# Attention maxima of a head: rounded and split on GpSimd, turned later, copied by ScalarE

## The chip, the cores and the metric

The kernel runs on one core of a Trainium2 chip. Its time is that of one execution on the device, in microseconds (us); lower is better. The engines are called as the profile calls them: PE (TensorE; PEld is its loading of weights), DVE (VectorE), ACT (ScalarE), POOL (GpSimd) and SP (SyncE, which here only issues transfers).

## The reference

A block of a transformer on one sequence of 2048 tokens with 448 features: a layer norm modulated by a condition, attention with 16 heads of 28 features, and behind it a gated MLP with a mixing of the tokens. Only the attention is touched.

```
q, k, v = heads of h @ wqkv                 # 16 heads, 2048 x 28 each
scores  = (q @ k^T) * 28 ** -0.5            # 2048 x 2048 for each head
p       = exp(scores - max) / sum           # softmax over the keys
o       = p @ v
x       = x + ga * (o @ wo)
```

## The kernel before

The attention goes head by head, and within a head over 16 key tiles of 128 keys, two at a time (a *pair*, function `pair`). The scores are made with the keys on the partitions and 512 queries on the columns (`s_mm`, tile `st_ps`), ACT turns them into `P` by an exponential, and PE multiplies `P` with `V` (`pv_mm`, tile `o_ps`) one pair later. What has to be known before a head's scores are taken is the greatest score of each query, since the exponential works on score minus maximum.

These maxima are made about 20 key tiles ahead (`LEAD`). For each block of 128 queries, `m_mm` makes the product with 512 keys (tile `mt`) and DVE reduces it to one column of `pm` (L754). In heads 1 to 13 (`RAW`) the first 512 queries go another way: their scores are made with the keys on the partitions (`r_mm`, tile `rt`), ACT copies them to SBUF as raw tiles (`rawA`, `rawB`, `rawC`), DVE folds them into a running maximum `rmax` (L801), and `r_turn` turns that by PE and reduces it into the first four columns of `mxv` (L809). Once the maxima are known, `r_neg` (L813, L817) spreads them over the partitions as `rneg`, POOL adds it to the raw tiles (`r_sub`, L820), and ACT takes the exponential from there.

`m_max` finishes a head: one reduction of `pm` gives the negated maxima `mxv` (128 x 16), and three more write their rounded part and the remainder (`mxp`, both in a type with fewer bits for PE). `m_fin` turns `mxp` by PE (L775, tile `mtp`), DVE copies the 32 x 128 result to `nt` (L778), and SP sends it into rows 84 and 85 of `qst`, the query operand of the scores, so that the product with the keys comes out with the maximum already subtracted. POOL has work beside this: sums of blocks of the mixing weights (`ws_op`, L957 and L952), whose loads and stores go through SP.

Each engine works in the order in which the program writes its instructions. That order is written out by hand: `ORDERS` has one letter for each step of a pair (r raw score, p products with V, s score, m maximum product, | the events of the second key tile), and tables `events` and `late` hold what is run at a key tile: `events` of the first tile at the pair's start, `late` of it right behind the products with V. A planner (`Clock`) with estimates of how long a bank of PSUM is held chooses the bank of each product.

`m_max` and `m_fin` of head h stand at key tile 16h - 4 of the whole row of tiles, that is, two pairs ahead of the head's own first tile. In a head after 13, `m_fin` stood one tile later in `events`.

Of the kernel before, what the change touches and what calls it, by code (L numbers as in the profile page):

```python
# [8 lines left out]
F32 = mybir.dt.float32  # L9
F32R = mybir.dt.float32r  # L10
AF = mybir.ActivationFunctionType
ALU = mybir.AluOpType
AX = mybir.AxisListType
# [6 lines left out]
NT = S // 128  # L20
# [67 lines left out]
def tile_adaln_mha_gmlp(ctx, tc, x, wqkv, wo, w_in, w_spT, b_sp, w_out, cT, w_mod, out):  # L88
    nc = tc.nc
    ctx.enter_context(tc.manual_schedule())  # L90
    pe, dve, act, pool, sp = nc.tensor, nc.vector, nc.scalar, nc.gpsimd, nc.sync
# [48 lines left out]
    def sub(eng, dst, a, hi):  # L140
        eng.tensor_tensor(out=dst, in0=a, in1=hi.bitcast(F32), op=ALU.subtract)  # L141
# [101 lines left out]
    def bank(name):  # L243
        k = mode[0](name) if mode[0] else banks[0]
        banks.remove(k)
        banks.append(k)
        return ring.tile([128, 512], F32, name=name, tag=f"b{k}")
# [6 lines left out]
    def load_mod(pair, eng):  # L254
        for k in range(4):
            n = 2 * D if k < 3 else 512
            wms[pair, k] = wm = e1.tile([128, 2 * D], F32, name="wm", tag=("wm", "wm", "raw")[pair], bufs=4)[:, :n]
            eng.dma_start(wm, w_mod[:, pair, 2 * D * k : 2 * D * k + n])
            if k < 3:
                wms[pair, k] = wm.rearrange("p (a b) -> p a b", b=D)  # L260
# [43 lines left out]
    for r0, r1, a, o in ((0, 128, 0, 3), (0, 64, 3, 1), (64, 128, 3, 1)):  # L304
        b = a + r0 // 64
# [239 lines left out]
    order = [(0, 0), (0, 3), (2, 2), (2, 5), (1, 1), (3, 0), (1, 4), (5, 2), (4, 1), (6, 6), (6, 7)]  # L545
# [103 lines left out]
    for g in range(1, NG):  # L649
        if g == 3:  # L650
# [4 lines left out]
            npool = att.enter_context(tc.tile_pool(name="npool", bufs=2))  # L655
# [73 lines left out]
    RAW = range(1, 14)  # L729
# [13 lines left out]
    pms = {}  # L743

    def m_mm(j, kb):
        h, t = divmod(j, NT)
        mt = bank("mt")
        pe.matmul(  # L748
            mt, qst[h % 3][:, t * 128 : (t + 1) * 128], kst[h % 3][:, kb * 512 : (kb + 1) * 512], start=True, stop=True
        )  # L750
        if h not in pms:
            pms[h] = npool.tile([128, NT, 4], F32, name="pm")
        clock.read("dve", 0.598)
        dve.tensor_reduce(out=pms[h][:, t, kb : kb + 1], in_=mt, axis=AX.X, op=ALU.max)  # L754

    mxs = {}

    def m_max(h):

        r = 4 if h in RAW else 0  # L760
        if h not in mxv:
            mxv[h] = npool.tile([128, NT, 2], F32, name="mxv")
        mx = mxv.pop(h)
        clock.spend("dve", 0.5)
        dve.tensor_reduce(out=mx[:, r:, 0], in_=pms.pop(h)[:, r:, :], axis=AX.X, op=ALU.max, negate=True)
        mxs[h] = npool.tile([128, 2, NT], F32R, name="mxp")
        dve.tensor_reduce(out=mx[:, :, 1].bitcast(F32R), in_=mx[:, :, 0:1], axis=AX.X, op=ALU.max, negate=True)
        dve.tensor_reduce(out=mxs[h][:, 0, :], in_=mx[:, :, 0:1], axis=AX.X, op=ALU.max)
        with nc.allow_low_precision(reason="the low part of a split, as the other splits write it"):
            dve.tensor_reduce(out=mxs[h][:, 1, :], in_=mx, axis=AX.X, op=ALU.add)  # L770

    def m_fin(h):
        mx = mxs.pop(h)
        tp = bank("mtp")
        pe.transpose(tp[0 : 2 * NT, 0:128], mx.bitcast(F32).rearrange("p a b -> p (a b)"), ident)  # L775
        nt = npool.tile([2 * NT, 128], F32, name="nt", bufs=1)
        clock.read("dve", 0.3)
        dve.tensor_copy(nt, tp[0 : 2 * NT, 0:128])  # L778
        sp.dma_start(qst[h % 3][84:86, :].bitcast(F32), nt[:, :])

    mxv, seen, rmax, rneg = {}, [], [], []
# [6 lines left out]
    def r_mm(u):  # L788
        st = score("rt", *divmod(u, NT), 0)
        b = clock.read("act", 0.477, hold=u % NT > 0)  # L790
        act.activation(raw_tile(u), st, AF.Copy)  # L791
        if u % NT:
            seen.append((u, st, b))

    def r_max():
        while seen:
            u, st, b = seen.pop(0)
            if not rmax:
                rmax.append(stage2.tile([128, 512], F32, name="rmax", tag="ql"))
            clock.read("dve", 0.6, *b)  # L800
            dve.tensor_tensor(out=rmax[0], in0=st, in1=raw_tile(u - 1) if u % NT == 1 else rmax[0], op=ALU.max)  # L801

    def r_turn(h):
        tp = bank("rtp")
        for t in range(4):
            pe.transpose(tp[:, t * 128 : (t + 1) * 128], rmax[0][:, t * 128 : (t + 1) * 128], ident)  # L806
        mxv[h] = npool.tile([128, NT, 2], F32, name="mxv")
        clock.read("dve", 0.62)
        dve.tensor_reduce(out=mxv[h][:, 0:4, 0], in_=tp.rearrange("p (a b) -> p a b", b=128), axis=AX.X, op=ALU.max, negate=True)  # L809

    def r_neg(h):
        st = bank("st_ps")
# [19 lines left out]
    def s_mm(u, qb):  # L832
        st = score("st_ps", *divmod(u, NT), qb)
        clock.ready[u] = clock.read("act", 0.477)[1]
        s_exp(u, qb, st)

    def x_exp(u):
        clock.ready[u] = clock.spend("act", 0.477)
        s_exp(u, 0, raw_tile(u))
# [4 lines left out]
    def pv_mm(u):  # L844
        h, kt = divmod(u, NT)
        if kt == 0:
            otile[h] = ps_o.tile([128, 512], F32, name="o_ps", tag="o")
        for qb in range(4):
            pe.matmul(  # L849
                otile[h][32 * qb : 32 * qb + 32, :], V[:, kt, h, :], ptiles.pop((u, qb)), start=kt == 0, stop=kt == NT - 1  # L850
            )
# [120 lines left out]

    LEAD = 20
    NU = H * NT
    events, late = {}, {}

    def at(slot, fn, *a, when=events):
        when.setdefault(slot, []).append((fn, a))

    for h in range(H):  # L980
        if h >= 2:
            at(h * NT - LEAD - 10, load_head, h)
        e0 = (h + 1) * NT
        at(e0 + 1, n_copy, h)
        at(e0 + 2, n_sum, h)
        at(e0 + 4, n_recip, h)
        at(e0 + 6, n_bcast, h)
        at(e0 + 8, n_mul, h)
        at(e0 + 9, n_scatter, h)
        at(h * NT + NT - LEAD, m_max, h)  # L990
        at(max(h * NT + NT - LEAD, -2) + (h > RAW[-1]), m_fin, h, when=events if h > RAW[-1] else late)
    for h in RAW:
        at(h * NT - 6, r_turn, h, when=late)
        at(h * NT - 1, r_neg, h)
# [74 lines left out]
    def m_first():  # L1069
        j, kb = first[done[0]]  # L1070
        m_mm(j, kb)
        done[0] += 1
        if done[0] >= 4 * NT and kb == 3:
            for when in (events, late):
                for e in [e for e in sorted(when) if e <= j - 3 - LEAD]:
                    for fn, a in when.pop(e):
                        fn(*a)
# [33 lines left out]
    def run(when, u):  # L1111
        for fn, a in when.pop(u, []):
            fn(*a)

    ORDERS = {6: "rrpm|smsmssmsmsm", 8: "rrpm|smmsmmsmsmsm"}

    def pair(u):
        ss = [[(v, qb) for qb in range(1 if v // NT in RAW else 0, 4)] if v < NU else [] for v in (u, u + 1)]
        S_, M_, R_ = ss[0] + ss[1], m_work[u] + m_work[u + 1], r_work[u] + r_work[u + 1]
        X_ = [v for v in (u, u + 1) if v < NU and v // NT in RAW]  # L1120
        xat = [len(R_)] * 2
        if X_:
            order = ORDERS[8 if len(M_) > 6 else 6]
        else:
            lead = 1 if M_ else 4
            order = "r" * len(R_) + "s" * lead + "p" + "ms" * (4 - lead) + "|" + "ms" * 4 + "m" * len(M_)
        n_o = 0

        def exps():
            while X_ and n_o >= xat[-len(X_)]:  # L1130
                x_exp(X_.pop(0))

        run(events, u)
        exps()
        for c in order + "s" * len(S_) + "r" * len(R_) + "m" * len(M_):
            if c == "p":
                if u > 0:
                    pv_mm(u - 2)
                    pv_mm(u - 1)
                    clock.pause((u - 2, u - 1))  # L1140
                run(late, u)
            elif c == "|":
                run(events, u + 1)
            elif c == "s" and S_:
                s_mm(*S_.pop(0))
                n_o += 1
                exps()
            elif c == "r" and R_:
                r_mm(R_.pop(0))
                n_o += 1  # L1150
                exps()
                if not R_:
                    r_max()
            elif c == "m" and M_:
                m_mm(*M_.pop(0))
        assert not X_ and not seen
        run(late, u + 1)
# [102 lines left out]
    h = H - 1  # L1260
# [310 lines left out]
    for s in range(2):  # L1571
        for six in (False, True):
            prev = None
            for n in [n for n in range(s, NP, 2) if PRODUCTS[n][1] or not six]:
                c, _, new, _ = PRODUCTS[n]
# [184 lines left out]
    order = free[0:3] + [free[6]] + free[3:6]  # L1760
# [68 lines left out]
```

## Time and profile before

| | us |
|---|---|
| median of 3 runs | 1352.79 |
| lowest, highest | 1352.58, 1353.44 |
| the profiled execution | 1353.0 |
| its span, first to last instruction | 1351.2 |

| engine | busy us in the span | share |
|---|---|---|
| PE | 1344.5 | 100% |
| DVE | 1082.2 | 80% |
| ACT | 908.5 | 67% |
| POOL | 604.2 | 45% |

The attention's pairs run from about 151 us to 837 us of the span. A matmul's end is modelled in these records, so that PE counts as busy even in short waits; where it waits is seen from the starts of its instructions and from the idle time of the weight loads. Figures in brackets at a row's end are idle time of that engine just before, and what ended it.

### The profile page before, as it was taken

How to read it: one execution, taken by the hardware profiler on the slowest of the kernel's cores; microseconds unless marked ns; L12 is line 12 of the kernel's file. 1: busy time of each engine (PE TensorE's matmuls, PEld its weight loads, DVE VectorE, ACT ScalarE, POOL GpSimd, SP SyncE). 2: the span in 40 equal slices, each digit the busy share in tenths (PEclk: the TensorE clock that was granted, in tenths of full speed). 3: DMA queues.
4: the chain of work that ended last, by engine and by line, in shares of the span. 5: the costliest groups of instructions: out<-in, count | busy, mean ns of one | idle time of the engine just before them, and what ended most of it. 6: DMA issues, size and time to landing. Idle time of an engine off the chain costs nothing.

```text
span 1351.2 us, 20695 instructions
## 1 busy us (share of the span) xinstructions
PE 1344.5 (100%) x6945; PEld 939.2 (70%) x6945; DVE 1082.2 (80%) x1777; ACT 908.5 (67%) x1687; POOL 604.2 (45%) x521
## 2 busy tenths in 40 slices
PE   9999999999999999999999999999999999999998
PEld 8888655555555555555555555988998888888898
DVE  7798889999999999999999960851379798889582
ACT  6623789999999999999997779363234653444221
POOL 2134428987888779788787761100141000000000
PEclk9999999999999999999999999999999999999999
DMA  8465614455345525553434222533102443435842
GB/s 296 135 175 181 211 57 127 135 150 150 112 121 151 144 86 136 146 155 109 113 80 119 83 80 66 189 119 136 63 9 89 125 114 102 118 103 178 269 157 82
DMA packets 92870, 174.68 MB, mean 129 GB/s; under 512 B 16536, under 2 KB 31770, under 8 KB 90218
## 3 DMA queue, kind: packets, MB, share of 16 engines
q1 hardware_dynamic: 90046, 169.06, 41.7%
q10 hardware_dynamic: 2718, 4.30, 0.9%
q8 instruction: 55, 0.90, 0.3%
q14 instruction: 51, 0.42, 0.1%
HBM read 111.71 MB, written 56.82 MB: 125 GB/s over the span
## 4 chain that ended last, share of the span: by engine, by line
PE 97%; DVE 2%; ACT 0%; issue 0%; POOL 0%; DVEq 0%; ACTq 0%
PE acc L1605 19%; PE o_ps L849 17%; PE mt L748 15%; PE st_ps L785 14%; PE z_ps L1497 5%; PE z_ps L1329 5%; PE pq L413 4%; PE rt L785 4%; PE wo_ps L1194 3%; PE y_ps L1685 2%; PE y_ps L1683 2%; PE pv L395 2%; PE y_ps L1684 2%; DVE pm L754 1%; PE rtp L806 1%; PE tp L191 1%
## 5 line engine op out<-in xcount | busy, mean ns | idle before, releaser
L754 DVE TENSOR_REDUCE pm<-mt 128x1 f32<-128x512 f32 x816 | 506.7, 681 | 16.6 <-PE mt L748 16.4
L830 ACT ACTIVATE P<-st_ps 128x512 f32<-128x512 f32 x816 | 420.7, 618 | 52.0 <-PE st_ps L785 49.7
L748 PE MATMUL mt<-kst,qst 128*128 128x512 f32 x816 | 331.0, 410 | 1.0 <-DVE rmax L801 0.7
L785 PE MATMUL st_ps<-qst,kst 128*128 128x512 f32 x816 | 298.6, 401 | 0.0
L849 PE MATMUL o_ps<-P,V 128*32 128x512 f32 x2048 | 247.3, 598 | 0.0
L748 PEld LDWEIGHTS mt<-kst,qst 128*128 128x128 f32 x816 | 153.2, 188 | 113.1 <-issue 40.4
L1605 PE MATMUL acc<-wsp_h,heapA 128*128 128x512 f32 x752 | 231.6, 389 | 0.0
L785 PEld LDWEIGHTS st_ps<-qst,kst 128*128 128x128 f32 x816 | 152.3, 188 | 51.9 <-DVE pm L754 7.8
L820 POOL TENSOR_TENSOR rawA<-rawA,rneg 128x512 f32<-128x512 f32 x126 | 160.3, 1292 | 43.9 <-ACT rneg L817 43.9
L957 POOL TENSOR_TENSOR ws_raw<-ws_raw 128x512 f32<-128x512 f32 x124 | 159.7, 1291 | 20.8 <-DMA ws_scr<-ws_raw 16.7
L1605 PEld LDWEIGHTS acc<-wsp_h,heapA 128*128 128x128 f32 x752 | 141.2, 188 | 29.1
L1385 ACT ACTIVATE wsp_h<-raw_sp 128x512 fp32r<-128x512 f32 x104 | 65.6, 632 | 125.5 <-PE acc L1605 112.4
L1605 PE MATMUL acc<-wsp_l,heapA 128*128 128x512 f32 x376 | 146.3, 389 | 0.0
L801 DVE TENSOR_TENSOR rmax<-rt,rmax 128x512 f32<-128x512 f32 x182 | 124.7, 685 | 25.3 <-ACT rawA L791 8.5
L849 PEld LDWEIGHTS o_ps<-P,V 128*32 128x32 f32 x2048 | 57.1, 109 | 114.2 <-issue 103.1
L820 POOL TENSOR_TENSOR rawB<-rawB,rneg 128x512 f32<-128x512 f32 x64 | 81.6, 1292 | 35.8 <-ACT rneg L817 35.8
L141 DVE TENSOR_TENSOR wsp_l<-raw_sp,wsp_h 128x512 fp32r<-128x512 f32 x104 | 70.3, 685 | 16.6 <-ACT wsp_h L1385 16.4
L1605 PEld LDWEIGHTS acc<-wsp_l,heapA 128*128 128x128 f32 x376 | 70.6, 188 | 14.7
L830 ACT ACTIVATE P<-rawA 128x512 f32<-128x512 f32 x126 | 75.9, 676 | 0.0
L791 ACT ACTIVATE rawA<-rt 128x512 f32<-128x512 f32 x126 | 71.9, 649 | 0.0
L785 PE MATMUL rt<-qst,kst 128*128 128x512 f32 x208 | 69.0, 413 | 0.0
L413 PE MATMUL pq<-heapD,heapD 128*128 128x512 f32 x196 | 61.8, 390 | 0.0
(259 smaller groups left out, 1819.4 us busy)
## 6 DMA issues: line engine op xcount, KB each, us to landing
ws_scr<-ws_raw SPq DMA_DIRECT2D x92, 256.0 KB
raw_sp<-ws_scr SPq DMA_DIRECT2D x92, 256.0 KB
ws_raw<-in_w_spT_dram SPq DMA_DIRECT2D x72, 256.0 KB
kst<-qk_scr SPq DMA_DIRECT2D x45, 224.0 KB
qst<-qk_scr SPq DMA_DIRECT2D x45, 224.0 KB
qk_scr<-qh SPq DMA_DIRECT2D x28, 256.0 KB
qk_scr<-ql SPq DMA_DIRECT2D x28, 256.0 KB
z_scr<-z1t SPq DMA_DIRECT2D x28, 256.0 KB
```

The lines of the kernel that those rows point to most:

```text
L141: eng.tensor_tensor(out=dst, in0=a, in1=hi.bitcast(F32), op=ALU.subtract)
L413: pe.matmul(pq, wqk[:, b, m * 128 : (m + 1) * 128], hT[g][:, a, :], start=j == 0, stop=j == NST - 1)
L748: pe.matmul(mt, qst[h % 3][:, t * 128 : (t + 1) * 128], kst[h % 3][:, kb * 512 : (kb + 1) * 512], start=True, stop=True)
L754: dve.tensor_reduce(out=pms[h][:, t, kb : kb + 1], in_=mt, axis=AX.X, op=ALU.max)
L785: pe.matmul(st, kst[h % 3][:, kt * 128 : (kt + 1) * 128], qst[h % 3][:, qb * 512 : (qb + 1) * 512], start=True, stop=True)
L791: act.activation(raw_tile(u), st, AF.Copy)
L801: dve.tensor_tensor(out=rmax[0], in0=st, in1=raw_tile(u - 1) if u % NT == 1 else rmax[0], op=ALU.max)
L820: pool.tensor_tensor(out=raw_tile(u), in0=raw_tile(u), in1=rneg[0], op=ALU.add)
L830: act.activation(p, src, AF.Exp, scale=SCALE)
L849: pe.matmul(otile[h][32 * qb : 32 * qb + 32, :], V[:, kt, h, :], ptiles.pop((u, qb)), start=kt == 0, stop=kt == NT - 1)
L957: pool.tensor_tensor(out=ws_tile(op[0]), in0=ws_tile(op[2]), in1=ws_tile(op[4]), op=ALU.add if op[3] == "+" else ALU.subtract)
L1605: pe.matmul(a[j], z[:, c], w, start=start and k == 0, stop=st == 3 and k == 2, skip_group_check=not new or j == 3)
```

## The change

The reduction of `pm` to `mxv` stays on DVE. The rounding and the remainder become two operations of POOL (a copy into the rounded type and a subtraction). `m_fin` runs at a new mark, `!`, in the order of a pair, which stands five products behind the products with V; its copy of the turned rows is made by ACT. The estimates of the planner are set to that.

```
         dve.tensor_reduce(out=mx[:, r:], in_=pms.pop(h)[:, r:, :], axis=AX.X, op=ALU.max, negate=True)
         mxs[h] = npool.tile([128, 2, NT], F32R, name="mxp")
-        dve.tensor_reduce(out=mx[:, :, 1].bitcast(F32R), in_=mx[:, :, 0:1], axis=AX.X, op=ALU.max, negate=True)
-        dve.tensor_reduce(out=mxs[h][:, 0, :], in_=mx[:, :, 0:1], axis=AX.X, op=ALU.max)
-        with nc.allow_low_precision(reason="the low part of a split, as the other splits write it"):
-            dve.tensor_reduce(out=mxs[h][:, 1, :], in_=mx, axis=AX.X, op=ALU.add)
+        pool.tensor_copy(mxs[h][:, 0, :], mx)
+        sub(pool, mxs[h][:, 1, :], mx, mxs[h][:, 0, :])
...
-        clock.read("dve", 0.3)
-        dve.tensor_copy(nt, tp[0 : 2 * NT, 0:128])
+        clock.read("act", 0.25)
+        act.activation(nt, tp[0 : 2 * NT, 0:128], AF.Copy)
...
-        at(max(h * NT + NT - LEAD, -2) + (h > RAW[-1]), m_fin, h, when=events if h > RAW[-1] else late)
+        at(max(h * NT + NT - LEAD, -2), m_fin, h, when=mids)
...
-    ORDERS = {6: "rrpm|smsmssmsmsm", 8: "rrpm|smmsmmsmsmsm"}
+    ORDERS = {6: "rrpm|smsm!ssmsmsm", 8: "rrpm|smms!mmsmmsmsm"}
...
+            elif c == "!":
+                run(mids, u)
```

On PE, at the maxima of head 11 (`mtp` is the turn, `mt` the products for maxima of the head after, `st_ps` scores, `o_ps` the products with V). Before:

```order
L849 MATMUL o_ps<-P,V 32x512 x8
L775 MATMUL mtp<-ident,mxp 32x128
L748 MATMUL mt<-kst_870,qst_871 128x512
L785 MATMUL st_ps<-qst_873,kst_872 128x512
L748 MATMUL mt<-kst_870,qst_871 128x512
L785 MATMUL st_ps<-qst_873,kst_872 128x512
L748 MATMUL mt<-kst_870,qst_871 128x512
L785 MATMUL st_ps<-qst_873,kst_872 128x512 x2
```

With the change (the lines of the file have moved by two):

```order
L847 MATMUL o_ps<-P,V 32x512 x8
L748 MATMUL mt<-kst_870,qst_871 128x512
L783 MATMUL st_ps<-qst_873,kst_872 128x512
L748 MATMUL mt<-kst_870,qst_871 128x512
L783 MATMUL st_ps<-qst_873,kst_872 128x512
L748 MATMUL mt<-kst_870,qst_871 128x512
L773 MATMUL mtp<-ident,mxp 32x128
L783 MATMUL st_ps<-qst_873,kst_872 128x512 x2
```

The turn has moved from the place right behind the products with V to one five products later.

On POOL, at the same place. Before:

```order
L820 TENSOR_TENSOR rawA<-rawA,rneg 128x512 x2
L820 TENSOR_TENSOR rawB<-rawB,rneg 128x512
L957 TENSOR_TENSOR ws_raw<-ws_raw 128x512 x6
L820 TENSOR_TENSOR rawB<-rawB,rneg 128x512 x6
L957 TENSOR_TENSOR ws_raw<-ws_raw 128x512
```

With the change:

```order
L818 TENSOR_TENSOR rawA<-rawA,rneg 128x512 x2
L818 TENSOR_TENSOR rawB<-rawB,rneg 128x512
L955 TENSOR_TENSOR ws_raw<-ws_raw 128x512 x3
L767 CAST mxp<-mxv 128x16
L141 TENSOR_TENSOR mxp<-mxv,mxp 128x16
L955 TENSOR_TENSOR ws_raw<-ws_raw 128x512 x3
L818 TENSOR_TENSOR rawB<-rawB,rneg 128x512 x6
```

The two new operations stand in the middle of six sums of weights, behind everything that POOL was given for earlier key tiles.

On SP, around the transfer of `nt` of that head. Before:

```order
L890 DMA heapD_90<-osb 24x512 x4
L949 DMA ws_scr<-ws_raw 128x512
L779 DMA qst_875<-nt 2x16x128
L949 DMA ws_scr<-ws_raw 128x512 x4
L955 DMA ws_raw<-in_w_spT_dram 128x512
```

With the change:

```order
L888 DMA heapD_90<-osb 24x512 x4
L947 DMA ws_scr<-ws_raw 128x512 x4
L777 DMA qst_875<-nt 2x16x128
L947 DMA ws_scr<-ws_raw 128x512
L953 DMA ws_raw<-in_w_spT_dram 128x512
```

The transfer of `nt` now stands behind three more stores of weight sums.

More of the change, by code (lines that the diff above doesn't have):

```diff
@@ L761, in m_max @@
         if h not in mxv:
-            mxv[h] = npool.tile([128, NT, 2], F32, name="mxv")
+            mxv[h] = npool.tile([128, NT], F32, name="mxv")
         mx = mxv.pop(h)
-        clock.spend("dve", 0.5)
-        dve.tensor_reduce(out=mx[:, r:, 0], in_=pms.pop(h)[:, r:, :], axis=AX.X, op=ALU.max, negate=True)
+        clock.spend("dve", 0.21)
+        dve.tensor_reduce(out=mx[:, r:], in_=pms.pop(h)[:, r:, :], axis=AX.X, op=ALU.max, negate=True)
         mxs[h] = npool.tile([128, 2, NT], F32R, name="mxp")
-        dve.tensor_reduce(out=mx[:, :, 1].bitcast(F32R), in_=mx[:, :, 0:1], axis=AX.X, op=ALU.max, negate=True)
-        dve.tensor_reduce(out=mxs[h][:, 0, :], in_=mx[:, :, 0:1], axis=AX.X, op=ALU.max)
-        with nc.allow_low_precision(reason="the low part of a split, as the other splits write it"):
-            dve.tensor_reduce(out=mxs[h][:, 1, :], in_=mx, axis=AX.X, op=ALU.add)
+        pool.tensor_copy(mxs[h][:, 0, :], mx)
+        sub(pool, mxs[h][:, 1, :], mx, mxs[h][:, 0, :])
     def m_fin(h):
@@ L806, in r_turn @@
             pe.transpose(tp[:, t * 128 : (t + 1) * 128], rmax[0][:, t * 128 : (t + 1) * 128], ident)
-        mxv[h] = npool.tile([128, NT, 2], F32, name="mxv")
+        mxv[h] = npool.tile([128, NT], F32, name="mxv")
         clock.read("dve", 0.62)
-        dve.tensor_reduce(out=mxv[h][:, 0:4, 0], in_=tp.rearrange("p (a b) -> p a b", b=128), axis=AX.X, op=ALU.max, negate=True)
+        dve.tensor_reduce(out=mxv[h][:, 0:4], in_=tp.rearrange("p (a b) -> p a b", b=128), axis=AX.X, op=ALU.max, negate=True)
     def r_neg(h):
@@ L974, in tile_adaln_mha_gmlp @@
     NU = H * NT
-    events, late = {}, {}
+    events, late, mids = {}, {}, {}
     def at(slot, fn, *a, when=events):
@@ L1073, in m_first @@
         if done[0] >= 4 * NT and kb == 3:
-            for when in (events, late):
+            for when in (events, late, mids):
                 for e in [e for e in sorted(when) if e <= j - 3 - LEAD]:
@@ L1113, in run @@
             fn(*a)
-    ORDERS = {6: "rrpm|smsmssmsmsm", 8: "rrpm|smmsmmsmsmsm"}
+    ORDERS = {6: "rrpm|smsm!ssmsmsm", 8: "rrpm|smms!mmsmsmsm"}
     def pair(u):
@@ L1125, in pair @@
             lead = 1 if M_ else 4
-            order = "r" * len(R_) + "s" * lead + "p" + "ms" * (4 - lead) + "|" + "ms" * 4 + "m" * len(M_)
+            order = "r" * len(R_) + "s" * lead + "p" + "ms" * (4 - lead) + "|" + "msms!msms" + "m" * len(M_)
         n_o = 0
```

## The prediction

> **What bounds the kernel now.** I read the page first (busy shares), then cut the attention stretch by head and by pair of key tiles, then read one pair instruction by instruction. The columns of the windows are: stretch, its length, and the busy time of PE, PEld, DVE, ACT and POOL in it.
>
> ```profile
> PE 1344.5 (100%) x6945; PEld 939.2 (70%) x6945; DVE 1082.2 (80%) x1777; ACT 908.5 (67%) x1687; POOL 604.2 (45%) x521
> ```
> ```profile
> 279.80:323.50 43.70, 43.70 (x248) 23.84 (x247) 41.01 (x72) 41.09 (x82) 36.45 (x30) 1.00 0.53 151
> ```
> ```profile
> 303.26:308.54 5.28, 5.28 (x32) 2.93 (x31) 5.02 (x9) 5.08 (x11) 2.81 (x3) 1.00 0.50 141
> 308.54:314.29 5.75, 5.75 (x36) 3.27 (x35) 4.68 (x9) 5.16 (x11) 5.75 (x6) 1.00 0.43 135
> 314.29:320.12 5.83, 5.83 (x33) 2.73 (x32) 5.66 (x14) 5.50 (x12) 4.43 (x4) 1.00 0.14 50
> 320.12:325.61 5.49, 5.49 (x33) 3.15 (x32) 5.38 (x10) 4.92 (x11) 2.19 (x2) 1.00 0.87 272
> 325.61:331.17 5.56, 5.56 (x32) 3.06 (x31) 4.94 (x9) 5.56 (x13) 5.56 (x6) 1.00 0.35 108
> ```
>
> The second row is one head (43.7 us), in which DVE and ACT are each busy 41: whole-kernel shares of 80% and 67% hide that. The third group is five successive pairs of it. A plain pair takes 5.28. The pair that makes the maxima of head 4 (314.29) takes 5.83, the next one 5.49, of which one matmul (L813) is 0.23.
>
> ```profile
> 305.11 0.50 PE L748 MATMUL mt<-kst,qst 128*128 128x512 f32 x1
> 305.45 0.40 PE L785 MATMUL st_ps<-qst,kst 128*128 128x512 f32 x1
> 307.98 0.63 PE L785 MATMUL rt<-qst,kst 128*128 128x512 f32 x2
> ```
>
> A plain pair is bound by PE: products with V for 1.85 (a pair starts with them, here at 303.26, and the first key tile's product stands at 305.11), 0.34 for the first score, then 0.23 each (305.45 to 307.98 is eleven steps), and the next products at 308.54. So DVE work is worth something only where PE waits for it, and a wait put into PE's order is paid in full.
>
> ```profile
> 315.40 0.20 DVE L765 TENSOR_REDUCE mxv<-pm 128x12 f32<-128x48 f32 x1
> 315.64 0.17 DVE L767 TENSOR_REDUCE mxv<-mxv 128x16 fp32r<-128x16 f32 x1
> 315.94 0.68 DVE L801 TENSOR_TENSOR rmax<-rt,rawA 128x512 f32<-128x512 f32 x1
> 316.14 0.28 PE L775 MATMUL mtp<-ident,mxp 128*32 128x128 f32 x1
> 317.34 0.27 DVE L778 COPY nt<-mtp 32x128 f32<-32x128 f32 x1
> 317.54 3.66 DVE L754 TENSOR_REDUCE pm<-mt 128x1 f32<-128x512 f32 x6
> 318.86 0.19 PEld L785 LDWEIGHTS st_ps<-qst,kst 128*128 128x128 f32 x1 [0.30 <-DVE pm L754]
> 316.93 3.22 ACT L830 ACTIVATE P<-st_ps 128x512 f32<-128x512 f32 x6 [0.30 <-PE st_ps L785]
> 322.31 0.40 PE L813 MATMUL st_ps<-qst,ones 128*128 128x512 f32 x1
> 322.74 0.60 ACT L817 ACTIVATE rneg<-st_ps 128x512 f32<-128x512 f32 x1 [0.57 <-PE st_ps L813]
> ```
>
> In the maxima pair PE does wait for DVE (the row with 0.30 is one of several). That, 5.83 against 5.28, is the 0.55 that there is to win.
>
> **The change part by part.** *DVE.* Three of four small reductions go: 315.94 - 315.64 = 0.30. The copy of the turned rows goes: 317.54 - 317.34 = 0.20. Together 0.50 per head. PE's own turn stays (about 0.05), so 0.50 is the ceiling of the gain in a pair.
>
> *ACT.* It gets the copy of 32x128. No such row exists on ACT; the nearest is the small copy L387, 0.24, and DVE's own is 0.27: I take 0.25.
>
> ```profile
> L387 ACT ACTIVATE xn<-xn 128x64 f32<-128x64 f32 x4 | 0.9, 244 | 0.1
> L900 POOL CAST heapO<-heapD 128x512 fp32r<-128x512 f32 x12 | 7.3, 611 | 0.0
> L967 POOL CAST ws_raw<-ws_raw 128x448 fp32r<-128x448 f32 x7 | 3.9, 557 | 0.5
> L968 POOL TENSOR_TENSOR ws_raw<-ws_raw 128x448 f32<-128x448 f32 x7 | 8.1, 1153 | 0.6
> L957 POOL TENSOR_TENSOR ws_raw<-ws_raw 128x512 f32<-128x512 f32 x124 | 159.7, 1291 | 20.8 <-DMA ws_scr<-ws_raw 16.7 <-PE rt L785 1.4 <-DMA ws_raw<-in_w_spT_dram 0.2
> L164 POOL TENSOR_SCALAR rsz<-mvz 128x1 f32<-128x1 f32 x16 | 9.3, 579 | 105.5 <-DMA raw_sp<-ws_scr 64.6 <-DVE mvz L1503 40.9
> ```
>
> ACT idles 0.30 and 0.57 in the two pairs above and not at all in the third (5.56 of 5.56). Pairs shorter by 0.50 and 0.25 more work eat 0.75 of those 0.87, so some of the gain comes back as late reads of PSUM. I take 0.35 per head as what is left, between 0.10 (a copy's whole 0.25 and the rest lost) and 0.50. In heads 13 and 14 the raw columns have ended and ACT has room: 0.50 there.
>
> *POOL's two operations.* From 512 to 448 columns a rounding loses 54 ns and a subtraction 138, which leaves 0.19 and 0.22 at 16 columns; with 0.1 allowed for the wait of the second for the first, 0.5 in all, and 0.1 to reach PE. Ends for the range: 0.1 less, and 0.58 each by L164, the tiny operation that runs slowest, which is 0.7 more. I take 0.5, since kind and neighbours are those of L967 and L968.
>
> On this the Trainium skill, GPSIMD Engine Reference, section 4.1 Engine selection, advises against the move: two-input elementwise work is put at about half VectorE's speed on GPSIMD. The L957 row agrees in kind (1.29 against 0.68 for L801, which reads PSUM); at 16 columns the fixed part decides, and by an estimate from the page's factor of two on L767's 0.17 the two would cost 0.7, which is 1 us more over the five heads below.
>
> *When POOL gets to them.* This is the term that decides. POOL works in order, and the two operations stand behind the additions to the raw columns (L820) and to the weights (L957, L952) of earlier slots. Row pairs: the last POOL operation ahead of the new ones, then the first addition with the next head's rneg (R); heads 3, 4, 6, 10, 11, 12.
>
> ```profile
> 271.34 1.50 POOL L952 TENSOR_SCALAR ws_raw<-ws_raw 128x512 f32<-128x512 f32 x1
> 279.63 1.30 POOL L820 TENSOR_TENSOR rawA<-rawA,rneg 128x512 f32<-128x512 f32 x1 [5.53 <-ACT rneg L817]
> 316.19 1.29 POOL L957 TENSOR_TENSOR ws_raw<-ws_raw 128x512 f32<-128x512 f32 x1
> 323.42 1.30 POOL L820 TENSOR_TENSOR rawB<-rawB,rneg 128x512 f32<-128x512 f32 x1 [4.70 <-ACT rneg L817]
> 404.67 1.30 POOL L957 TENSOR_TENSOR ws_raw<-ws_raw 128x512 f32<-128x512 f32 x1
> 411.03 1.30 POOL L820 TENSOR_TENSOR rawA<-rawA,rneg 128x512 f32<-128x512 f32 x1 [3.69 <-ACT rneg L817]
> 580.27 1.30 POOL L957 TENSOR_TENSOR ws_raw<-ws_raw 128x512 f32<-128x512 f32 x1
> 586.26 1.30 POOL L820 TENSOR_TENSOR rawC<-rawC,rneg 128x512 f32<-128x512 f32 x1 [3.45 <-ACT rneg L817]
> 624.54 1.29 POOL L957 TENSOR_TENSOR ws_raw<-ws_raw 128x512 f32<-128x512 f32 x1
> 630.00 1.29 POOL L820 TENSOR_TENSOR rawB<-rawB,rneg 128x512 f32<-128x512 f32 x1 [0.20 <-ACT rneg L817]
> 667.11 1.29 POOL L957 TENSOR_TENSOR ws_raw<-ws_raw 128x512 f32<-128x512 f32 x1
> 673.81 1.29 POOL L820 TENSOR_TENSOR rawA<-rawA,rneg 128x512 f32<-128x512 f32 x1 [3.83 <-ACT rneg L817]
> ```
>
> In head 4 the old turn stands at 316.14, right behind the products with V. Five tiles later is 0.34 + 4 x 0.23 = 1.25 later. PE waits from then on for whatever POOL lacks, and all scores behind the turn wait with it: ACT and DVE run dry, SP holds the transfer of nt.
>
> Where POOL is late, its chain sets the time: end of the old operation + 0.6, then the way from the turn to R. That way is nine matmuls (2.07), the turn and the switch (0.15), products with V (1.85), a first score (0.34), then 323.42 - 322.31 = 1.11 from L813 to R: 5.5. So R moves by (end + 6.1 - R):
> - head 3: 272.84 + 6.1 - 279.63 = -0.7, POOL is no obstacle;
> - head 4: 317.48 + 6.1 - 323.42 = +0.2;
> - head 6: 405.97 + 6.1 - 411.03 = +1.0;
> - head 10: 581.57 + 6.1 - 586.26 = +1.4;
> - head 11: 625.83 + 6.1 - 630.00 = +1.9;
> - head 12: 668.40 + 6.1 - 673.81 = +0.7.
>
> Sum +5.2 in five heads (the gain of those heads is already in it). Heads 1, 2, 5, 7, 8 and 9 have POOL free no later than head 3 does, and 13 and 14 find it idle.
>
> *SP.* nt now goes out behind the stores of two slots. It is late only in head 11:
>
> ```profile
> 624.22 0.67 SPq L779 DMA_DIRECT2D qst<-nt  x1
> 624.99 3.79 SPq L949 DMA_DIRECT2D ws_scr<-ws_raw  x3
> ```
>
> The third store issued until 628.78 because it waits for POOL; with 0.5 more ahead of it nt goes at about 629.3, and L813 is due at 626.4 + 4.4 = 630.8. Before there were 4.7 (317.63 to 322.31 in head 4) without a wait shown. Cost between 0 and 3.2; I take 0.3, since the issue itself is 0.67 and the rest of 1.5 should nearly do.
>
> *Sum.* -7 x 0.35 - 2 x 0.50 = -3.5; +5.2 + 0.3; the first and the last head change nothing, their turn has room. Net about +2.1. The profiled execution took 1353.0 (span 1351.2), 0.2 over the median 1352.79: 1352.8 + 2.1 = **1354.9 us**, +0.15%.
>
> **The rivals.** *POOL is in time.* If POOL reaches the operations within 1.15 us of the reduction in all heads (1.75 from the reduction's end at 315.60 to the new place of the turn, less 0.6), nothing waits and 12 heads win 0.35 to 0.50, two 0.50: 5 to 7 us, 1346 to 1348. For it: the lateness comes from one execution, and POOL's spans are rough. Against: POOL's rows have no gap of a microsecond ahead of these places, and nothing that the change does shortens its queue. 0.25.
>
> *ACT takes the gain.* The 0.25 goes onto the tightest engine; if every head's gain of 0.35 is lost, -3.5 falls to -1.0: 1357.4. It decides where ACT's reads leave PE without a free bank in the pair after the copy. 0.10.
>
> *Small operations on POOL are dear.* With L164's 0.58 each, five heads lose 0.7 more: 1358.4. 0.09.
>
> *DVE is held by POOL.* DVE's six reductions took 3.66 at 317.54 while POOL added until 318.72, so I see none of it; if DVE stood for POOL's 0.5, the whole DVE gain would go: 1358.4. The Trainium skill, Perfetto Trace Analysis, section Optimizing Scalar/DVE Operations, warns of it: the two share an SBUF port, so moving work between them might not help. 0.03.
>
> *The trade is even*, no wait and no gain: 1352 to 1353.5. 0.05.
>
> **How the numbers follow.** The forecast has 0.48; its own range is 1351 to 1358, from 0.10 and 0.50 of gain per head and 0.3 of POOL's lateness either way in five heads. Below 2.7 us (0.2%, about what a measurement tells from no change) of either sign lies 0.28 of it, 0.18 above, 0.02 below. With the rivals: faster 0.27, same 0.33, slower 0.40. The range 1348 to 1359 leaves out most of the first rival.
>
> **What would show it.** The new turn in heads 6, 10, 11 and 12 should show PE idle 1 to 2.5 us for POOL's mxp, none in heads 2, 5, 8; maxima pairs of about 5.4 to 5.5 there; POOL's pair 0.5. It is wrong if no wait for POOL stands on PE (then faster), or if pairs without one still take 5.8.

## The result, and the profile after

| | before | with the change |
|---|---|---|
| median | 1352.9 | 1361.6 |
| lowest, highest | 1352.6, 1353.4 | 1360.2, 1363.6 |
| the profiled execution | 1353.0 | 1361.2 |
| its span | 1351.2 | 1359.4 |

The ratio is 1.0065, with a 95% interval of 1.0052 to 1.0077: slower by some 8.7 us. (In the diff above, the second new string of `ORDERS` reads `rrpm|smms!mmsmsmsm` in the program.)

The page's line of busy times says nothing of it, as it said little before: DVE has 7 us less, ACT 2 more, POOL 6 more. The chain of work that ended last does: POOL has 8% of it, and DMA 4%. Below are the page's line of busy times and the chain with the change, and then the chain before.

```profile
PE 1344.0 (99%) x6945; PEld 940.3 (69%) x6945; DVE 1075.0 (79%) x1713; ACT 910.8 (67%) x1703; POOL 610.3 (45%) x553
...
PE 82%; POOL 8%; DMA 4%; issue 2%; ACT 2%; DVE 2%; SPq 1%; POOLq 0%; DVEq 0%; ACTq 0%
```
```profile
PE 97%; DVE 2%; ACT 0%; issue 0%; POOL 0%; DVEq 0%; ACTq 0%
```

I laid the pairs of both traces beside each other, one by one. In both the attention begins at 151 us, and it ends 7.9 us later than before. Where they went:

| pairs | change against before, us |
|---|---|
| maxima pairs of heads 1-5, 7-9, 13, 14 | -2.7 |
| maxima pairs of heads 6, 10, 11, 12 | +4.0 (+0.76, +1.15, +1.67, +0.41) |
| the pair behind the maxima, heads 4, 5, 6, 9, 10, 11, 12 | +5.4 (+1.10, +0.21, +0.53, +1.06, +1.06, +0.73, +0.69) |
| the pair ahead of the maxima, 0.07 each | +0.7 |
| all others | +0.6 |

The windows of the changed kernel: heads 4 (maxima pair and the next), 8 (maxima pair), and 11 (both). Columns as in the prediction.

```profile
313.84:319.42 5.58, 5.58 (x32) 2.92 (x31) 5.44 (x10) 5.22 (x12) 3.41 (x5) 1.00 0.56 192
319.42:326.02 6.60, 5.78 (x33) 3.15 (x32) 5.11 (x10) 5.12 (x11) 2.20 (x2) 1.00 0.40 120
491.41:497.00 5.59, 5.59 (x32) 2.92 (x32) 5.45 (x10) 5.24 (x12) 1.75 (x4) 1.00 0.22 79
625.68:633.18 7.50, 5.58 (x32) 2.91 (x31) 5.63 (x11) 5.34 (x12) 6.57 (x8) 1.00 0.20 76
633.18:639.61 6.43, 5.77 (x32) 3.15 (x32) 5.09 (x10) 5.27 (x11) 3.75 (x4) 1.00 0.43 125
```

A maxima pair without a wait takes 5.58 where it took 5.83. Head 4 wins that, and gives back four times as much one pair later (6.60, before 5.49). Head 11 loses in both. Two waits answer for this, each named by the view of one line: the turn (L773) waits for POOL's split, and the product that makes `rneg` (L811, L813 before) waits for a transfer.

```profile
L773 PE MATMUL mtp<-ident,mxp x16: 270/271/285, 137.7 to 809.2; 128*32 128x128 f32 x16
...
  POOL mxp L141: 5.0, 4
```
```profile
L811 PE MATMUL st_ps<-qst,ones x13: 389/497/505, 191.3 to 724.1; 128*128 128x512 f32 x13
...
  DMA qst<-nt: 9.6, 13
```

(The first names total and times for PE; the second adds up PE and its weight loads, which wait together.) Head 4, in order of time:

```profile
315.55 0.22 POOL L767 CAST mxp<-mxv 128x16 fp32r<-128x16 f32 x1
315.85 0.22 POOL L141 TENSOR_TENSOR mxp<-mxv,mxp 128x16 fp32r<-128x16 f32 x1
316.04 1.64 SPq L947 DMA_DIRECT2D ws_scr<-ws_raw  x2
317.50 0.25 ACT L776 ACTIVATE nt<-mtp 32x128 f32<-32x128 f32 x1
317.72 0.95 SPq L953 DMA_DIRECT2D ws_raw<-in_w_spT_dram  x2
318.76 0.69 SPq L777 DMA_DIRECT2D qst<-nt  x1
...
322.60 0.19 PEld L811 LDWEIGHTS st_ps<-qst,ones 128*128 128x128 f32 x1 [1.14 <-DMA qst<-nt]
322.60 0.50 PE L811 MATMUL st_ps<-qst,ones 128*128 128x512 f32 x1 [0.82 <-DMA qst<-nt]
```

POOL is in time here (its pair takes 0.52, the turn stood at 316.98). `nt` is copied by 317.75, but SP, which had stood at the second store, has just gone on to two loads of the next key tile: it issues `nt` at 318.76, 1.0 late. Behind these loads the transfer itself takes longer too, 2.8 from its issue to its last packet instead of 1.8. Before, SP issued it at 317.63, as soon as the copy had ended, and the loads came behind it:

```profile
317.63 0.69 SPq L779 DMA_DIRECT2D qst<-nt  x1
```

Head 11 has both waits:

```profile
626.38 4.01 POOL L955 TENSOR_TENSOR ws_raw<-ws_raw 128x512 f32<-128x512 f32 x3 [0.61 <-DMA ws_scr<-ws_raw]
626.79 0.20 DVE L765 TENSOR_REDUCE mxv<-pm 128x12 f32<-128x48 f32 x1
...
629.08 4.72 SPq L947 DMA_DIRECT2D ws_scr<-ws_raw  x3
630.34 0.20 POOL L767 CAST mxp<-mxv 128x16 fp32r<-128x16 f32 x1
630.61 0.22 POOL L141 TENSOR_TENSOR mxp<-mxv,mxp 128x16 fp32r<-128x16 f32 x1
630.79 4.02 POOL L955 TENSOR_TENSOR ws_raw<-ws_raw 128x512 f32<-128x512 f32 x3
630.89 0.28 PE L773 MATMUL mtp<-ident,mxp 128*32 128x128 f32 x1 [1.92 <-POOL mxp L141]
631.21 0.27 ACT L776 ACTIVATE nt<-mtp 32x128 f32<-32x128 f32 x1 [1.79 <-PE mtp L773]
633.88 0.69 SPq L777 DMA_DIRECT2D qst<-nt  x1
636.20 0.50 PE L811 MATMUL st_ps<-qst,ones 128*128 128x512 f32 x1 [0.66 <-DMA qst<-nt]
```

The maxima were ready at 626.99, and POOL came to them at 630.34 since three sums of weights stood ahead. `nt` was ready at 631.48, and SP came to it at 633.88, since it held a store that waits for sums of POOL behind the split. (The time of the changed kernel also spreads over 3.4 us, that of before over 0.9.)

### The profile page after: what moved, and what is told of

Its sections match the earlier page's. It is cut to its first block, busy times and chain, and to the rows that moved or that the text cites. A ratio compares the mean times of both kernels' runs of the same rounds, so it can differ in the third digit from the quotient of the medians.

```text
span 1359.4 us, 20687 instructions
## 1 busy us (share of the span) xinstructions
PE 1344.0 (99%) x6945; PEld 940.3 (69%) x6945; DVE 1075.0 (79%) x1713; ACT 910.8 (67%) x1703; POOL 610.3 (45%) x553
## 4 chain that ended last, share of the span: by engine, by line
PE 82%; POOL 8%; DMA 4%; issue 2%; ACT 2%; DVE 2%; SPq 1%; POOLq 0%; DVEq 0%; ACTq 0%
PE acc L1605 19%; PE o_ps L847 13%; PE mt L748 11%; PE st_ps L783 11%; PE z_ps L1497 5%; PE z_ps L1329 5%; PE pq L413 4%; POOL ws_raw L955 3%; PE wo_ps L1194 3%; PE rt L783 2%; POOL rawA L818 2%; DMA ws_scr<-ws_raw 2%; PE y_ps L1683 2%; PE y_ps L1685 2%; PE y_ps L1684 2%
```

## The experiments

Each time stands beside runs of the kernel before on the same chip, with medians from 1352.6 to 1353.1. Two theories stood against each other. *Two waits*: the late split costs about 4, and `nt` behind the next tile's loads and stores on SP costs 5.4, whether the split is late or not. *One wait*: all follows from the late split.

**SP's order put right.** In a maxima pair the second tile's steps run behind the turn, so that `nt` is issued first:

```
             elif c == "|":
-                run(events, u + 1)
+                if u not in mids:
+                    run(events, u + 1)
             elif c == "!":
                 run(mids, u)
+                run(events, u + 1)
```

> The changed kernel, but in a pair with maxima the events of its second key tile (loads, stores and additions) are issued behind the turn and the transfer of nt instead of ahead of them; POOL's own order stays. Theory A (two separate waits: POOL late with mxp, about 4.0 us in the maxima pairs of heads 6, 10, 11, 12; and nt late on SP behind the next tile's transfers, 5.4 us in the pairs behind the maxima): the second wait goes, about 1356 us (1355.5 to 1357.5), PE's wait for the transfer qst<-nt from 9.6 us to under 1, the first wait stays. Rival B (one wait: all of it follows from the late mxp): within 1 us of the changed kernel, 1360.5 to 1362.5.

Measured 1355.6 (1354.0 to 1358.9), ratio 1.0020 [1.0012, 1.0029]. Some 6 of the 8.7 us are gone with the order of one transfer. The pair behind the maxima of head 11 takes 5.50 (5.69 before the change, 6.43 with it), while the maxima pair still stands for POOL:

```profile
620.86:628.74 7.88, 5.58 (x33) 2.91 (x32) 5.63 (x11) 5.33 (x12) 6.92 (x8) 1.00 0.08 28
628.74:634.24 5.50, 5.50 (x33) 3.15 (x32) 5.09 (x10) 5.28 (x12) 3.77 (x4) 1.00 0.69 237
```

No wait for `qst<-nt` is left on PE. The late heads are now 3, 6, 11 and 12 (+0.67, +0.78, +2.05, +0.26), and 10 is in time: POOL's lateness moves when transfers move.

**SP's order made wrong in the kernel before.** The sharper test of the same term: nothing of the change but where `nt` is sent.

```
+        if h in RAW:
+            unsent.append((h, nt))
+        else:
+            m_send(h, nt)
+
+    def m_send(h, nt):
         sp.dma_start(qst[h % 3][84:86, :].bitcast(F32), nt[:, :])
...
             elif c == "|":
                 run(events, u + 1)
+                while unsent:
+                    m_send(*unsent.pop(0))
```

> The kernel before, in which one thing alone is changed: in heads 1 to 13 the transfer of nt is written behind the steps of the pair's second tile, that is, behind its loads and stores on SP, as the change does. Turn, copy and reductions stay as before. If SP's order is the larger cause: 1356 to 1364, and PE waits for qst<-nt at the pair behind the maxima. If nt would have been in time but for the late turn: 1352.5 to 1353.5.

Measured 1360.9 (1359.1 to 1364.1), ratio 1.0065 [1.0052, 1.0079]: as slow as the whole change, with no work of POOL added and the turn at its old place. The pair behind the maxima of heads 4 and 11, and head 11 in order of time:

```profile
319.48:326.59 7.11, 5.74 (x32) 3.15 (x31) 5.41 (x10) 4.93 (x11) 2.20 (x2) 1.00 0.41 128
630.02:637.84 7.82, 5.74 (x32) 3.15 (x31) 5.39 (x10) 4.93 (x12) 4.97 (x5) 1.00 0.40 129
```
```profile
627.24 0.27 DVE L778 COPY nt<-mtp 32x128 f32<-32x128 f32 x1
627.64 4.30 SPq L957 DMA_DIRECT2D ws_scr<-ws_raw  x3
632.03 0.69 SPq L785 DMA_DIRECT2D qst<-nt  x1
634.46 0.47 PE L821 MATMUL st_ps<-qst,ones 128*128 128x512 f32 x1 [2.08 <-DMA qst<-nt]
```

`nt` is ready at 627.51, 3.3 into its pair as before, and lies for 4.5 us behind three stores. All of the loss in the attention, 6.8 of 6.9, is in this pair of five heads (4, 6, 10, 11, 12).

**The turn at its old place**, the rest of the change kept (`m_fin` again right behind the products with V, ahead of the second tile's steps):

> The changed kernel, but with the turn, the copy and the transfer of nt back at their old place, right behind the products with V; POOL's part and ScalarE's copy stay. Theory A: PE meets POOL 1.25 us earlier, so nearly every head waits (sum of POOL's lateness over heads 2 to 12 about 17 us, less some 6 of DVE's waits that it covers), while nt stands ahead of the next tile's transfers and is not late there: 1361 to 1366 us, PE waiting for mxp in most heads, for the transfer in none. Rival B: the later place is what costs, 1354 to 1357 us.

Measured 1366.6 (1363.2 to 1368.4), ratio 1.0094 [1.0080, 1.0107], 0.6 above the range of theory A. The turn then waits for POOL in nearly all heads (maxima pairs +12.3 in sum, +4.36 in head 11), and PE no longer waits for `nt`, which goes out 0.03 behind its copy in every head. So the late place buys time for POOL and costs SP's order.

**The split on DVE by a copy and a subtraction**, the rest kept:

```
-        pool.tensor_copy(mxs[h][:, 0, :], mx)
-        sub(pool, mxs[h][:, 1, :], mx, mxs[h][:, 0, :])
+        dve.tensor_copy(mxs[h][:, 0, :], mx)
+        sub(dve, mxs[h][:, 1, :], mx, mxs[h][:, 0, :])
```

> The changed kernel, but the rounding and the subtraction are done by DVE instead of POOL (two operations of 128x16); the turn's place, ScalarE's copy and the order on SP stay. Theory A: mxp is never late, but nt still goes out behind stores that wait for POOL's sums, so that most of what the maxima pairs win is lost again one pair later: 1359 to 1361 us, and PE's wait for the transfer grows in head 11. Rival B: without POOL in the chain both waits go: 1353 to 1354.5 us.

Measured 1369.2 (1368.5 to 1372.0), ratio 1.0123 [1.0109, 1.0137]: both theories missed, and it was no clean undoing. The copy takes 174 ns where nothing runs beside it, and up to 1187:

```profile
L767 DVE CAST mxp<-mxv x16: 174/363/1187, 135.1 to 815.1; 128x16 fp32r<-128x16 f32 x16
L141 DVE TENSOR_TENSOR mxp<-mxv,mxp x16: 174/176/1227, 135.3 to 815.3; 128x16 fp32r<-128x16 f32 x16
```
```profile
453.40 1.31 POOL L955 TENSOR_TENSOR ws_raw<-ws_raw 128x512 f32<-128x512 f32 x1
453.54 0.20 DVE L765 TENSOR_REDUCE mxv<-pm 128x12 f32<-128x48 f32 x1
453.77 0.97 DVE L767 CAST mxp<-mxv 128x16 fp32r<-128x16 f32 x1
```

The copy ends at 454.74, 0.03 behind POOL's addition (454.71), while the reduction ahead of it ran through under that same addition in its usual 0.20. The old split was made of reductions, and the change had to be undone with those.

**The split on DVE by the three old reductions**, the turn at its new place, ACT's copy and SP's order as in the change:

> The changed kernel with the three old reductions back on VectorE; the turn stays at its new place, ScalarE keeps the copy, SP's order is that of the change. (A clean undo of GpSimd's part: these reductions were never held up by GpSimd in the trace before, while the copy and subtraction on VectorE were.) Two waits: PE no longer waits for the split (-4.0 in heads 6, 10, 11, 12), but nt still stands behind the stores on SP (+5.4 against before): 1357 to 1360. One wait, everything following from GpSimd's lateness: 1352 to 1354.

Measured 1363.4 (1357.5 to 1365.1), ratio 1.0064 [1.0046, 1.0081]. PE waits no more for the split, all maxima pairs of heads 2 to 12 take 5.63 to 5.65, and the kernel is no faster than the change: the one-wait theory is out. The loss is 12.7 in the pairs behind the maxima, more than I expected, and 8.2 of it is in heads 11 and 12 (4.02 and 4.19). These show something new. First the product for `rneg` in this kernel's head 11, then the 4 us from there on, then the 4 us behind the turn in head 11 of the kernel with SP's order put right; the granted clock is the third column from the right:

```profile
633.88 0.80 PE L813 MATMUL st_ps<-qst,ones 128*128 128x512 f32 x1 [2.46 <-DMA qst<-nt]
```
```profile
633.88:637.88 4.00, 4.00 (x11) 3.19 (x12) 1.76 (x3) 2.65 (x5) 2.49 (x3) 0.60 0.32 72
```
```profile
626.45:630.45 4.00, 3.99 (x26) 2.05 (x26) 2.58 (x4) 3.65 (x8) 3.78 (x3) 1.00 0.36 131
```

Behind a wait of 2.46 PE ran 4 us at 0.60 of its clock, which by (1 - 0.60) x 4 is an estimated 1.6 us more; together they make about the 4.02 that this pair lost. In the other kernel, behind a wait of 2.30, the clock stayed at 1.00. The one execution of this kernel whose mean clock was 1.000 took 1357.5, within the range of the two-waits theory; the four with 0.997 took 1362.8 to 1365.1.

**Both waits out**: the three reductions on DVE, and SP's order put right. Of the change there remain the turn's place and ACT's copy.

> As the run before, and the steps of the pair's second tile run behind the turn in a maxima pair, so that SP gets nt ahead of the next tile's stores. Both waits are then out, and what is left of the change is the turn's new place and ScalarE's copy. Two waits: 1351.5 to 1353 (0.10 won in some ten maxima pairs, 0.07 lost in the pair ahead). If the turn's late place costs by itself, by whatever hangs on the maxima: above 1355.

Measured 1350.7 (1350.0 to 1351.2), ratio 0.9980 [0.9972, 0.9989]: faster than the kernel before, and below the range of the two-waits theory, since a maxima pair won 0.19 and not 0.10. Against the first experiment, which differs in the split alone, it is 4.9 faster: that is the price of the split on POOL with `nt` in time.

**The same with DVE's copy of `nt`**, so that only the turn's place remains:

> The run e6_both_out with VectorE's copy of nt in place of ScalarE's: of the change only the turn's new place is left. If place and copy share the gain of 2.4, as the pairs of e3_dve_copy say (0.10 of it by the copy in a pair): 1351.3 to 1352.3. If the place makes all of it: 1350.4 to 1351. If the copy makes all of it: 1353.

Measured 1353.1 (1352.5 to 1353.5), ratio 1.0003 [0.9994, 1.0012]: the place alone wins nothing, and in the kernel before this one all of the 2.4 came from a copy of 0.25 us a head moved from DVE to ACT. (ACT's copy with the turn at its old place and the split on DVE was not run.) The maxima pair of head 8, first of this kernel and then of the one with ACT's copy:

```profile
489.30:495.18 5.88, 5.88 (x33) 2.76 (x32) 5.71 (x14) 5.56 (x12) 1.88 (x2) 1.00 0.01 3
```
```profile
488.69:494.34 5.65, 5.65 (x32) 2.83 (x31) 5.48 (x13) 5.34 (x12) 1.92 (x2) 1.00 0.03 9
```

**ACT's copy undone in the changed kernel**:

> The changed kernel, but DVE copies the turned rows as before, at the new place. The prediction's ACT term (0.15 of the 0.50 that DVE wins per head is lost by ScalarE's 0.25) would give the 0.15 back and take DVE's 0.20: no more than 1 us either way, 1360.5 to 1362.5 us. If ScalarE's copy is what keeps the maxima pairs of heads 2, 3, 5, 7, 8 at 5.58 instead of 5.33, they fall to about 5.4 and the time to 1359.5.

Measured 1365.5 (1361.2 to 1365.7), ratio 1.0081 [1.0069, 1.0094], above what was expected. Maxima pairs without a wait take 5.68: beside the split on POOL the copy is worth only 0.10 in a pair. And `nt` is copied later yet, so that more is lost behind it (head 4: +1.99). The profiled execution was the lowest, 1361.2, so that what the others lost more is not seen; their mean clock was 0.999 against its 1.000, which is an estimated 1.4 us of 1365.

**A short queue on POOL.** To see the change without POOL's lateness, its sums of weights go over 16 of 512 columns (what the tokens are mixed with is then not the reference's; loads and stores are as before), once in the kernel before and once in the changed one.

```
-            t = ws_tile(op[1])
+            t = ws_tile(op[1])[:, 0:16]
...
-                out=ws_tile(op[0]), in0=ws_tile(op[2]), in1=ws_tile(op[4]), op=ALU.add if op[3] == "+" else ALU.subtract
+                out=ws_tile(op[0])[:, 0:16],
+                in0=ws_tile(op[2])[:, 0:16],
+                in1=ws_tile(op[4])[:, 0:16],
```

> The kernel before with GpSimd's sums of weights over 16 of 512 columns only (what it multiplies the tokens with is then not the reference's; loads and stores are as before), so that GpSimd's queue is short. As GpSimd makes no one wait in the trace before: 1352 to 1353.

> The changed kernel with the same short queue on GpSimd (the same part of the computation left out). If GpSimd's queue is behind both waits (the split late, and the stores ahead of nt late because they wait for the sums): nothing is late, each head wins 0.25 to 0.35 and the time is 2 to 4 below the run n0_light_pool_before. If SP's order costs even with the sums ready: 0 to 3 above it.

Measured 1352.6 for the kernel before (ratio 0.9999 [0.9990, 1.0008]) and 1350.2 for the changed one (0.9981 [0.9973, 0.9990]). With the sums short PE has neither wait, though the order on SP is the change's: stores whose sums are ready hold `nt` for 0.6 at most (head 10). So POOL's queue is the root of both waits, by two ways: directly, and through the stores on SP. All maxima pairs of heads 2 to 12 take 5.57 to 5.59:

```profile
488.37:493.94 5.57, 5.57 (x32) 2.91 (x31) 5.43 (x10) 5.21 (x12) 0.42 (x2) 1.00 0.09 32
```

Against 5.65 with the reductions on DVE and the copy on ACT, the split on POOL wins only 0.07 more in a maxima pair, even where POOL is free. It gives the same 0.07 back in the pair ahead, in each of heads 3 to 12. So in the end it wins nothing over the reductions on DVE: either kernel is 2.4 below the one that it was measured beside (1350.2 and 1350.7).

**The split on DVE in heads 3, 4, 6, 10, 11 and 12**, on POOL in the others, where it was in time, SP's order put right:

> As the run before, but GpSimd rounds and splits in the heads where it was not late (1, 2, 5, 7, 8, 9, 13, 14), and VectorE in heads 3, 4, 6, 10, 11, 12. Two waits: no wait for the split is left and eight heads win 0.25 instead of 0.10, so 1350 to 1352, below the kernel before. If GpSimd's lateness is not tied to these heads but moves with the transfers from program to program: 1353 to 1356, with waits for the split in other heads.

Measured 1350.1 (1349.7 to 1350.9), ratio 0.9978 [0.9969, 0.9987], no wait for the split. This is the best of all kernels here, but it can't be told from the one with the split all on DVE (1350.7), nor from the changed one with the short queue (1350.2).

## Why the prediction was wrong

The side (slower) had the largest of the three chances, 0.40, and the time lies 2.6 above the end of the range. By its steps:

- *SP: "It is late only in head 11", +0.3.* This step failed. It measured 5.4, in seven heads, and by itself (the kernel before with SP's order alone changed) even 6.8 in five. I had seen that `nt` would stand behind the stores of two slots, and looked at SP's wait for POOL in one head. In head 4 I set 4.7 us "without a wait shown" against a copy that comes 0.6 later in its pair (3.91 after its start, 3.32 before), and left out that SP is at that moment in the middle of 2.6 us of stores and loads. The order on SP was at hand for all heads; the wait of each of its stores could be read from the trace.
- *POOL's lateness, +5.2.* The mechanism, the heads and nearly the size held: +0.76, +1.15, +1.67 and +0.41 in heads 6, 10, 11 and 12 where the working gave +1.0, +1.4, +1.9 and +0.7; head 4, given as +0.2, was in time. That it came so near in each head is partly luck, since with other transfers it moved to other heads.
- *POOL's two operations, 0.5.* Held: 0.22 and 0.22 (0.20 and 0.22 in head 11), with 0.08 between. The estimate of 0.7 from the Trainium skill (GPSIMD Engine Reference, section 4.1 Engine selection) was too high here; its advice against two-input work on GpSimd held in another way, since POOL's long two-input sums made the small ones late.
- *The gain, 0.35 in seven heads and 0.50 in two.* It was 0.25 in a maxima pair, 0.51 in head 13 and 0.31 in head 14, and 0.07 was given back in the pair ahead of the maxima of heads 3 to 12. That loss stands in every kernel here with the split on POOL in all heads and in none with it on DVE; what makes it is not shown. I took the reductions' 0.30 and the copy's 0.20 as adding up. They do not: with the turn at its new place a pair takes 5.88; without the copy on DVE 5.65, without the reductions 5.68, without both 5.58. Either alone is worth 0.20 to 0.23, and the second one 0.07 to 0.10. What stops the pair at 5.57, with the short queue on POOL too, is not settled. "Wrong if pairs without one still take 5.8" didn't come true; they took 5.58, not the 5.4 to 5.5 foretold. PE still waits for DVE in such a pair; head 8 of the changed kernel:

```profile
494.55 0.27 PE L773 MATMUL mtp<-ident,mxp 128*32 128x128 f32 x1
495.07 0.25 ACT L776 ACTIVATE nt<-mtp 32x128 f32<-32x128 f32 x1
495.37 0.19 PEld L783 LDWEIGHTS st_ps<-qst,kst 128*128 128x128 f32 x1 [0.29 <-DVE pm L754]
```

- *ACT's copy, 0.25.* Held, 0.25. That ACT would take the gain did not come true; with DVE's reductions kept, ACT's copy made the whole gain.
- *The rivals.* POOL was not in time, its operations were not dear, and the trade was not even. A rival in which SP's queue holds `nt` in most heads was missing; the numbers for it stood in the range of one term (0 to 3.2, for one head).

The sum as it measured, in the attention: -2.7 + 4.0 + 5.4 + 0.7 + 0.6 = +8.0 (7.9 from the pairs' ends).

## What to carry to other kernels

When a step moves in program order, go through every queue that it passes, at every place where it happens: a small transfer behind a store that waits for a busy engine is late by that engine's backlog, and that was worth more here than the step itself. Before an operation of 0.2 us goes to an engine that works in pieces of 1.3, read how long that engine's queue is at the moment of need; its share of 45% doesn't say it. And make the parts of a change separately: the turn's new place with the copy on ACT, and the transfer kept first, wins 2.4 us, and the rest lost more than four times that.

## What the runs showed of the hardware

*DVE stands while POOL adds, if it copies, or works on two inputs, in SBUF.* A copy and a subtraction of 128 x 16 took 0.17 to 0.18 alone and up to 1.23 under a running addition of POOL, and ended about 0.03 behind it; the old reductions of the split took at most 0.19 beside POOL in the kernel before. The Trainium skill, SBUF — State Buffer, section Who interferes with whom, says so: a copy in a two-port mode and an operation with two inputs in SBUF contend with GpSimd, and on this chip a `tensor_reduce` never does. The runs agree for POOL's additions. For its operations with one input they leave it open: beside such a one the copy and the subtraction of head 3 were not held (below), but the copy of head 6 took 0.24 and the subtraction of head 14 took 0.58, and both ended 0.03 behind one.

```profile
273.12 1.49 POOL L950 TENSOR_SCALAR ws_raw<-ws_raw 128x512 f32<-128x512 f32 x1
273.91 0.17 DVE L767 CAST mxp<-mxv 128x16 fp32r<-128x16 f32 x1
274.12 0.17 DVE L141 TENSOR_TENSOR mxp<-mxv,mxp 128x16 fp32r<-128x16 f32 x1
```

The prediction gave a chance of 0.03 to a hold of DVE by POOL's own small split. That didn't come true: DVE's operations beside the split took their usual 0.68 to 0.69. What is held is a split on DVE written as a copy and a subtraction, by POOL's long sums.

*A long wait of PE costs twice.* Behind waits of PE of 2.33, 2.46, 2.62 and 3.33 us the granted clock of the next 4 us was 0.57 to 0.60, which is an estimated 1.6 to 1.7 us more; behind fourteen waits of 1.20 to 2.30 it stayed at 1.00. The Trainium skill, TensorE: Matmul & The Clock Gate, section Why this matters for your kernels, warns of gaps above some 3 us; here 2.33 was enough. In the profiled execution of the changed kernel no wait was longer than 1.92 and the clock stayed at 1.00, so this has no part in the 7.9 us of its trace. Two of its other three executions had a mean clock of 0.999; what waits they had is not seen.
